# Sixteen more products of zeros in a fused attention and MLP kernel, and its list of steps in another order

## The chip, the cores and the metric

The kernel runs on one core of a Trainium2 chip. The metric is the device time of one execution in microseconds (us), as a median over runs.

## The reference

Eight batches of eight heads, 576 positions, 64 columns a head. Causal attention with a bias from running sums of a gate, then a layer norm, an MLP with ReLU, and the sum:

```python
scores = scale * q @ k.T
cum = cumsum(maximum(s, 0))
scores = where(causal, -1e9, scores + minimum(-(cum[q] - cum[k]), 0))
attn = softmax(scores)
x = concat_heads(attn @ v)                 # 8 x 576 x 512
xn = (x - mean(x)) / sqrt(var(x) + 1e-6) * g_ln
out = x + maximum(xn @ w_ch1, 0) @ w_ch2   # 512 -> 2048 -> 512
```

## The kernel before

The bias is folded into the values: a key's weight is the exponential of its running sum, less a share of the last sum. The sums are scanned on VectorE (DVE), turned on TensorE (PE) and put through an exponential on ScalarE (ACT) into the tile `wt` (steps `relu`, `relur`, `scan`, `wr`, `wT`, `wx`; L244 to L257 and L892 to L920). Each v tile, 128 keys of all heads, is multiplied by it (`vm`, L212), on DVE or on GpSimd (POOL), and `vo` adds the weights themselves as two more columns, so that the row sums come out of the same product.

PE runs everything else as matrix products, in this order for a batch: q and k are brought into the form with the head's columns on partitions; scores of keys by queries, an exponential on ACT out of PSUM, the mask of the diagonal on POOL or in the product; the v products; division by the row sums on DVE. Then the rows of the batch are normalised (`ga` statistics, `la` the normalised tile on DVE), turned (`Da`, a transposing DMA), and multiplied by `w1` and, after ReLU, by `w2`. The last 64 rows of two batches make one mixed tile.

The order of all this is written out by hand, as a list of words, `PLAN` (from L1064), that a loop goes through (L1144). A word is a step with its numbers, and after a colon the engine: A for ACT, D for DVE, P for POOL, S for the SP queue. A step appends its instructions to the engines' queues; each engine works its queue in order and waits where data or a buffer is missing. So the list sets the order on each engine, and on each queue of DMAs: SP issues the v loads (`lv`), the row loads of later batches (`lr`) and the transposing DMAs; POOL issues the loads of pairs (`lp`, k then q, with a cast, L158) and of weights (`w1`, `w2`, 512 KB each, L233 to L240), between its own arithmetic. The words `U` and `u` take the next unit from a queue of MLP work (`run_units`, L691): four products of 512 columns, with the ReLU on DVE or on ACT; the first five units of batch 0 are pieces for one tile of rows. A unit is PE's filling work; there are 293 in both lists.

The start differs from the rest. Batches 0 to 2 are loaded as pairs of heads and turned on PE (`F.k.g`, `F.q.g` for pair g: 12 products, L276), then copied out of PSUM (`G`, L296). The pairs 0 to 3 are batch 0, and pair 0 comes through two f32 loads (`lf`, `cf`). Batch 0 is worked by tiles of queries: `S.t.n.mask` scores into two banks (L761), `x.t.n.i` the exponential (L789), `V.t.g` the v product for half of the heads (L807), `N` its division (L823), `B` and `L` statistics and normalised tile, `X` and `y` its transpose on PE and the copy, `M.c.t.j` a piece of the first MLP product with the weights of chunk c (L849), `r` its ReLU. `sd`, `se`, `sm` are the scores of the last 64 rows against themselves, their exponential on ACT and their mask on POOL (L375 to L398), `tk` the copy of the k tails for them, `me` a memset that it needs, `Z` the v products of the last rows. `fv` fills the tail of a v tile with zeros. From batch 1 on pairs are worked as bursts (`B2`, L402) with `bx`, `bm`, `Y` and `K` for exponential, mask, v products and division.

PSUM has eight banks. Up to the step `t6` two of them are `m` (pieces of the MLP), four `s` (scores) and two `t` (transposes of pairs and tiles, the turned sums, v products of batch 0). After `t6` there are two `m` (v products, outputs of the MLP) and six `s`. The step `W.n` (`keep_warm`, L704) lets PE multiply a tile of zeros n times, 512 columns each, into a bank that nobody reads:

Of the kernel before, what the change touches and what calls it, by code (L numbers as in the profile page):

```python
# [30 lines left out]
def fast_path(  # L31
# [672 lines left out]
    def keep_warm(n):  # L704
        w = ptile("t", [P, 512], "idle")
        for _ in range(n):
            nc.tensor.matmul(w, lhsT=zeros[:, 0:P], rhs=zeros, start=True, stop=True)
# [657 lines left out]
```

## Time and profile before

| What | us |
|---|---|
| median of three runs | 348.97 (348.58 to 349.32) |
| the profiled execution | 348.05 |
| its span, first to last instruction | 346.6 |
| PE busy in the span | 329.8 |

A profile is one execution. Engines are PE, PEld (the loading of weights into PE, which overlaps), DVE, ACT, POOL and SP; a q behind a name is its queue. A row of a timeline has the start, the busy time of the group, the engine, the line, the operation, what it writes and reads, the count, and in brackets the idle time ahead of it with what ended it. The granted clock is the share of full speed that the tensor engine's throttle let through.

### The profile page before, as it was taken

To read this page: it belongs to the slowest core of one execution; us is meant where nothing else is said; L and a number is where in the kernel's file an instruction comes from. 1 tells how busy PE (TensorE), PEld (TensorE's weight loads), DVE (VectorE), ACT (ScalarE), POOL (GpSimd) and SP (SyncE) were. 2 spreads that over 40 slices of the span, in tenths; PEclk is the share of its full clock that TensorE was granted. 3 is DMA by queue.
4 is the path that set the end of the run, shared out by engine and by line. 5 is a ranking of instruction groups with operands and counts; after the bars stand their busy time and mean duration, and the time that the engine had idled before them with its cause. 6 is when DMAs were issued, how large, how long until landed. Compare 5 with 4: busy or idle time off the path is not lost.

```text
span 346.6 us, 8106 instructions
## 1 busy us (share of the span) xinstructions
PE 329.8 (95%) x3143; PEld 178.2 (51%) x3169; DVE 223.0 (64%) x613; ACT 168.0 (48%) x312; POOL 146.9 (42%) x270
## 2 busy tenths in 40 slices
PE   5888899999999999999999999999999999999994
PEld 2667756555554555545554544554545444444443
DVE  3577859877698697747775768684867745025412
ACT  3685399775654667434762463363732202402500
POOL 6196968663777843664584173422240001000000
PEclk9569999999999999999999999999999999999998
DMA  8999999999999999889959924900140060021022
GB/s 161 207 198 224 207 204 206 178 204 261 169 207 253 195 213 229 181 186 199 230 151 206 220 46 109 220 25 2 62 121 3 0 166 32 0 77 61 1 60 65
DMA packets 140186, 49.76 MB, mean 144 GB/s; under 512 B 126000, under 2 KB 135984, under 8 KB 140144
## 3 DMA queue, kind: packets, MB, share of 16 engines
q1 hardware_dynamic: 130336, 40.69, 56.1%
q0 software_dynamic: 8880, 7.70, 13.9%
q10 hardware_dynamic: 928, 0.82, 0.9%
q8 instruction: 25, 0.41, 0.5%
q14 instruction: 17, 0.14, 0.1%
HBM read 37.11 MB, written 9.44 MB: 134 GB/s over the span
## 4 chain that ended last, share of the span: by engine, by line
PE 84%; DMA 4%; POOL 4%; DVE 3%; ACT 3%; issue 2%; POOLq 0%
PE py L629 35%; PE ph L610 34%; PE pot L442 5%; DMA qp<-in_q_dram 4%; PE sa L409 2%; ACT er L416 2%; PE sc L409 2%; PE pott L483 2%; PE sb L409 1%; POOL v_bf L215 1%; PE trp L289 1%; DVE v_bf L215 1%; ACT kq L138 1%; PE trp L282 1%; POOL kp L160 1%
## 5 line engine op out<-in xcount | busy, mean ns | idle before, releaser
L629 PE MATMUL py<-w_bf,hT 128*128 128x512 bf16 (+2 forms) x582 | 128.7, 367 | 2.2 <-issue 0.5
L610 PE MATMUL ph<-xT,w_bf 128*128 128x512 bf16 x480 | 109.2, 379 | 0.9 <-DVE hT L867 0.7
L602 ACT ACTIVATE hT<-ph 128x512 bf16<-128x512 f32 x78 | 46.8, 599 | 105.2 <-PE ph L610 104.1
L629 PEld LDWEIGHTS <-hT 128*128 128x128 bf16 x608 | 55.8, 98 | 60.0 <-DVE xb L461 0.3
L610 PEld LDWEIGHTS <-w_bf 128*128 128x128 bf16 x544 | 51.6, 98 | 58.8 <-issue 0.8
L353 POOL TENSOR_SCALAR_AFFINE_SELECT er<-er 128x256 bf16<-128x256 bf16 x112 | 46.5, 435 | 48.3 <-ACT er L416 34.3
L600 DVE TENSOR_SCALAR hT<-ph 128x512 bf16<-128x512 f32 x58 | 39.7, 688 | 25.0 <-PE ph L610 23.4
L641 DVE SCALAR_TENSOR_TENSOR yo<-py,rstd,xb 128x512 f32<-128x512 f32 x32 | 24.0, 749 | 37.5 <-PE py L629 28.7
L416 ACT ACTIVATE er<-sc 128x512 bf16<-128x512 f32 x56 | 33.3, 622 | 15.4 <-PE sc L409 15.1
L416 ACT ACTIVATE er<-sa 128x512 bf16<-128x512 f32 x56 | 33.8, 620 | 11.4 <-PE sa L409 11.0
L416 ACT ACTIVATE er<-sb 128x512 bf16<-128x512 f32 x56 | 33.8, 621 | 6.9 <-PE sb L409 4.9
L534 POOL TENSOR_TENSOR rstd<-rstd,mhalf 128x4 f32<-128x4 f32 (+1 forms) x8 | 9.2, 1145 | 48.2 <-DVE rstd L533 45.8
L215 POOL TENSOR_TENSOR v_bf<-rowtmp,wt 128x512 bf16<-128x512 f32 (+1 forms) x21 | 22.2, 1064 | 13.1 <-ACT wt L915 9.0
L442 PEld LDWEIGHTS <-er 128*128 128x128 bf16 x560 | 22.3, 97 | 9.7 <-DVE xb L461 0.9
L442 PE MATMUL pot<-v_bf,er 128*128 128x66 bf16 x560 | 25.3, 193 | 0.5 <-DVE xb L461 0.4
L200 POOL CAST kq<-rowtmp 128x512 bf16<-128x512 f32 (+1 forms) x30 | 19.5, 661 | 14.3 <-DMA rowtmp<-in_k_dram 14.3
L519 DVE BATCH_NORM_STATS2 stats<-xb 128x6 f32<-128x128 f32 (+1 forms) x84 | 24.8, 326 | 0.4
L461 DVE TENSOR_TENSOR xb<-pot,rinvs 128x256 f32<-128x256 f32 x56 | 23.8, 424 | 1.9
L560 DVE SCALAR_TENSOR_TENSOR xn<-xb,mv,gb 128x512 bf16<-128x512 f32 x28 | 22.9, 820 | 1.0
L409 PEld LDWEIGHTS <-kq 64*128 64x128 bf16 x448 | 14.3, 94 | 12.9 <-issue 6.7
L459 DVE TENSOR_REDUCE sums<-pot 128x4 f32<-128x8 f32 x56 | 8.8, 158 | 17.7 <-PE pot L442 17.2
L215 DVE TENSOR_TENSOR v_bf<-rowtmp,wt 128x512 bf16<-128x512 f32 (+1 forms) x19 | 17.4, 919 | 1.6 <-DMA rowtmp<-in_v_dram 1.6
(124 smaller groups left out, 320.3 us busy)
## 6 DMA issues: line engine op xcount, KB each, us to landing
rowtmp<-in_v_dram SPq DMA_DIRECT2D x32, 256.0 KB, 4.7
out_dram<-yo SPq DMA_DIRECT2D x32, 256.0 KB, 2.5
rowtmp<-in_k_dram SPq DMA_DIRECT2D x20, 256.0 KB, 4.0
rowtmp<-in_q_dram SPq DMA_DIRECT2D x20, 256.0 KB, 4.7
w_bf<-in_moe_w_ch_dram POOLq DMA_DIRECT2D x8, 512.0 KB, 9.9
kp<-in_k_dram POOLq DMA_DIRECT2D x11, 144.0 KB, 6.7
qp<-in_q_dram POOLq DMA_DIRECT2D x11, 144.0 KB, 7.0
rowtmp<-in_v_dram SPq DMA_DIRECT2D x8, 128.0 KB, 4.6
```

Source lines behind the costliest of these rows:

```text
L215: e.tensor_tensor(out=v_bf[b % 2][0:pn, t, :, 0:D], in0=loaded.pop(("v", b, t))[0:pn], in1=wt[0:pn, t, b, :].unsqueeze(2).to_broadcast([pn ...
L353: nc.gpsimd.affine_select(out=out, in_=out, compare_op=ALU.is_ge, fill=0.0, base=0, pattern=pattern, channel_multiplier=-1,)
L409: nc.tensor.matmul(a, lhsT=lhsT, rhs=rhs, start=True, stop=True)
L416: nc.scalar.activation(out=er[:, 2 * n % 4 + i, o : o + 512], in_=bank["B", n].pop((name, i)), func=ACT.Exp, scale=scale,)
L442: nc.tensor.matmul(pot[:, t, :], lhsT=e[:, o : o + P], rhs=v_bf[b % 2][:, kb, h, :], start=(kb == 0), stop=(kb == t),)
L461: nc.vector.tensor_tensor(out=xb[b][:, :, h * D : (h + 1) * D], in0=pot[:, :, 0:D], in1=rinv.unsqueeze(2).to_broadcast([P, NF, D]), op=ALU ...
L519: nc.vector.bn_stats(out=st[b][:, t, part, :], in_=x_tiles(b)[t][:, lo:hi])
L600: nc.vector.tensor_scalar_max(out=dst, in0=ph, scalar1=0.0)
L602: nc.scalar.activation(out=dst, in_=ph, func=ACT.Relu)
L610: nc.tensor.matmul(ph, lhsT=w1_bf[:, kd, fb * P : (fb + 1) * P], rhs=xT[:, :, kd, :], start=(kd == 0), stop=(kd == KD - 1),)
L629: nc.tensor.matmul(py[t], lhsT=hT[:, fb, t * P : (t + 1) * P], rhs=w2_bf[:, fb, c0:c1], start=(fb == 0), stop=(fb == FB - 1),)
L641: nc.vector.scalar_tensor_tensor(out=yo, in0=py[t], scalar=rs, in1=x[:, c0:c1], op0=ALU.mult, op1=ALU.add)
```

## The change

The bank of the zero product goes from `t` to `m`, and the list has another order. Beside W.9 there are now W.2 four times, W.3 once and W.1 five times, 16 products more. Some steps go to another engine: of the v tiles twelve words (`vm`, `vo`) go from POOL to DVE and eleven from DVE to POOL, several copies `G`, `y` and `O2` change between ACT and DVE, and four units have their ReLU on DVE instead of ACT. Otherwise both lists hold the same words. Shown are the lines of the list up to the first burst, with those of two of the transposing DMAs that are spoken of further on; the rest of the list changes its order in the same manner.

```diff
     def keep_warm(n):
-        w = ptile("t", [P, 512], "idle")
+        w = ptile("m", [P, 512], "idle")
         for _ in range(n):
             nc.tensor.matmul(w, lhsT=zeros[:, 0:P], rhs=zeros, start=True, stop=True)
...
     PLAN = """
-        f.0 mT c.0 I lf.k:S lf.q:A f.5 W.9 c.1 f.10 relur.2 relu.0 cf.q:D F.q.0 G.q.0:A lv.0.0:S O relur.1 lp.1
-        F.k.1 lp.2 f.2 scan.0 f.1 G.k.1:D cf.k:A qu.1 F.q.1 G.q.1:A F.k.0 G.k.0:A lv.0.1:S F.k.2 G.k.2:A S.1.0.1
-        lp.3 x.1.0.1 F.q.2 scan.1 scan.2 w1.1 wr F.k.3 G.q.2:A lv.0.3:S F.q.3 G.q.3:A wT wx vm.0.0:P g x.1.0.0
-        qu.2 G.k.3:D fv.0 S.0.0.1 S.1.1.1 x.0.0.0 vo.0:D w1.0 lv.0.2:S vm.0.1:D x.0.0.1 V.0.1 N.0.1 x.1.1.0
-        x.1.1.1 me B.0.1 S.2.0.1 S.4.0.0 V.1.0 N.1.0 V.0.0 tk.0 lv.0.4:S lv.1.0 x.2.0.0 x.4.0.1 N.0.0 x.4.0.0
-        x.2.0.1 S.4.1.0 x.4.1.0 lv.1.1 x.4.1.1 S.2.2.1 x.2.2.0 lp.7 vm.0.2:P qu.3 V.1.1 lv.1.3 qu.4 vm.0.3:P
-        S.2.1.1 lp.6 L.0 x.2.2.1 x.2.1.1 X.0 x.2.1.0 S.3.1.1 x.3.1.0 y.0:A B.1.0 S.3.0.1 x.3.0.1 V.2.0 vm.0.4:P
-        N.1.1 V.2.1 sd.0 L.1 X.1 N.2.1 x.3.1.1 S.3.3.1 M.0.0.0 lr.3.0 x.3.0.0 N.2.0 B.1.1 vm.1.0:P L.2 M.0.0.1
-        M.0.0.3 y.1:A M.0.1.0 lv.1.2 M.0.0.2 r.0.0:D V.3.0 N.3.0 M.0.1.2 S.3.2.1 A.1 lv.2.0 X.2 y.2:D se.0
-        M.0.1.3 x.3.3.1 M.0.1.1 M.0.2.2 r.0.1:D x.3.3.0 x.3.2.1 M.0.2.1 lp.4 B.0.0 M.0.2.3 x.3.2.0 M.0.2.0 V.3.1
-        N.3.1 L.3 r.0.2:A sm.0 Z.0 z.0 lp.5 F.k.4 F.q.4 w1.2 U G.k.4:A X.3 lp.8 F.k.6 y.3:D G.q.4:A w2.0 vo.1:P
-        B.2.0 G.k.6:A U u vm.1.1:P vm.1.3:D w1.3 cr.3.0.1 B.2.1 F.k.5 G.k.5:D La.3 F.q.5 G.q.5:D vm.1.2:P fv.1 U
-        u U u lp.9 t6 B.3.0 F.k.7 G.k.7:A lv.1.4 B.3.1 tk.1 F.q.6 G.q.6:D B2.4 A.0 bx.4.1 bx.4.3 w2.3 bx.4.0 U
...
-        cr.4.2.0 u u la.2.0 ga.2.0.3 bx.12.1 bm.12.1 cr.4.4.0 lv.4.1 bm.12.2 bm.12.3 se.3 la.2.3 Da.2.0 B2.13
...
-        bm.30.0 ga.6.1.2 la.6.2 U bx.30.3 bx.30.4 la.6.3 Da.6.0 U Y.29.1 K.29.1 B2.31 bx.31.3 u bx.31.2 bx.31.1
...
+        f.0 W.9 W.2 W.2 lf.k:S lf.q:A f.5 I c.1 lp.1 c.0 cf.k:A lv.0.1:S lv.0.0:S relur.2 fv.1 f.10 lp.2 me
+        F.k.1 f.2 O relur.1 cf.q:D F.q.0 lv.0.4:S W.3 F.q.1 F.k.2 relu.0 G.q.0:A W.1 G.q.1:A lv.0.2:S F.k.0
+        G.k.0:A W.1 scan.0 G.k.1:D lp.3 W.1 mT F.k.3 scan.1 lv.0.3:S G.k.2:D W.1 scan.2 G.k.3:A tk.0 lv.1.0
+        S.2.0.1 wr m F.q.2 wT G.q.2:D qu.1 wx g S.1.0.1 x.1.0.1 x.1.0.0 F.q.3 G.q.3:D w1.1 vo.0:D S.0.0.1
+        vm.0.3:D x.2.0.1 S.1.1.1 x.2.0.0 x.0.0.0 W.1 vm.0.1:P S.4.1.0 vm.0.0:D x.0.0.1 V.0.0 N.0.0 lv.1.3
+        x.1.1.0 x.1.1.1 V.1.0 w1.0 x.4.1.1 lp.4 x.4.1.0 V.0.1 S.4.0.0 N.1.0 lp.5 x.4.0.0 S.2.1.1 x.2.1.0 W.2
+        N.0.1 vm.0.2:P vm.1.0:P V.1.1 N.1.1 qu.2 L.1 x.2.1.1 B.1.1 x.4.0.1 L.0 S.3.0.1 V.2.0 x.3.0.0 W.2 S.2.2.1
+        x.3.0.1 X.1 lv.1.1 lr.3.0 qu.3 B.0.1 x.2.2.0 y.1:A sd.0 x.2.2.1 V.2.1 M.0.1.3 S.3.1.1 lv.1.2 x.3.1.0
+        M.0.1.1 N.2.0 f.1 X.0 se.0 sm.0 M.0.1.2 M.0.1.0 N.2.1 L.2 B.2.1 lp.6 B.1.0 F.q.4 G.q.4:D S.3.3.1 X.2
+        lv.1.4 y.0:A M.0.0.2 S.3.2.1 y.2:A M.0.2.3 fv.0 lp.8 r.0.1:A x.3.1.1 V.3.0 N.3.0 M.0.0.0 x.3.3.0
+        vm.0.4:P F.q.5 M.0.2.2 G.q.5:D x.3.3.1 x.3.2.1 M.0.0.3 x.3.2.0 M.0.2.0 V.3.1 lv.2.0 N.3.1 M.0.2.1
+        r.0.2:A M.0.0.1 r.0.0:D w1.2 F.k.6 G.k.6:A F.k.4 G.k.4:D B.2.0 L.3 Z.0 z.0 B.0.0 lp.7 cr.3.0.0 F.k.5
+        G.k.5:A u B.3.0 X.3 y.3:A vo.1:P u u u cr.3.0.1 A.0 u u U La.3 B.3.1 vm.1.2:D w1.3 vm.1.1:P t6 O2.q.8:D
+        F.q.7 F.k.7 G.q.7:A G.k.7:A B2.4 bx.4.1 lp.9 w2.1 A.3 U U w2.0 vm.1.3:D bx.4.0 vm.1.4:D bx.4.2 bx.4.3
...
+        bm.14.2 bm.13.3 K.12.1 bx.14.5 la.2.3 lr.4.2 cr.4.2.0 u U Da.2.0 lv.4.3 bx.14.1 bm.13.1 u sm.3 Y.13.0
...
+        bm.29.2 Y.29.0 bx.30.3 la.6.2 U U K.29.0 bx.30.5 bx.30.4 bx.30.2 u u u B2.31 bx.31.0 bx.31.2 la.6.0
+        la.6.3 Da.6.0 u u bx.31.4 bm.31.0 sm.7 bm.30.0 U U u bm.29.3 Y.29.1 bx.31.3 bx.31.5 K.29.1 ga.7.0.1
...
```

More of the change, by code (lines that the diff above doesn't have):

```diff
@@ new lines, in fast_path @@
+        vm.4.1:P U bm.15.0 u bm.15.2 lv.4.0 Y.14.0 K.14.0 Y.14.1 K.14.1 lr.5.0 lv.4.4 U vo.4:D u u u bm.15.1
+        Y.15.1 lv.5.2 qm lr.6.4 cr.5.2.1 lr.6.1 B2.16 bx.16.1 cr.5.4.0 lv.5.4 bx.16.0 sm.4 Z.3 ga.3.1.3 z.3
+        bx.16.3 bx.16.5 ga.3.0.0 bx.16.4 lv.5.0 u U cr.5.4.1 Y.15.0 K.15.0 K.15.1 ga.3.2.3 vm.4.0:P bx.16.2
+        bm.16.0 bm.16.2 cr.5.2.0 vo.5:D u ga.3.1.2 bm.16.3 vm.4.3:P u u lv.6.0 u ga.3.0.3 u ga.3.2.4 Y.16.0
+        bm.16.1 ga.3.1.1 lv.5.3 Da.1.4 B2.17 bx.17.1 bx.17.0 bx.17.3 Y.16.1 K.16.0 ga.3.1.0 bx.17.4 ga.3.1.4
@@ new lines, in fast_path @@
+        K.17.1 ga.4.0.0 lv.5.1 Y.18.1 U bm.19.2 U bx.19.1 u K.18.1 vm.5.0:P U lr.6.3 bm.19.0 lv.6.2 lv.6.1 u
+        Y.18.0 K.18.0 ga.4.0.1 Y.19.0 K.19.0 B2.20 lr.6.2 bx.20.1 Z.4 bx.20.4 vm.5.3:D lv.6.4 bx.20.2 la.3.4
+        bx.20.0 vm.5.1:D bm.19.1 bx.20.5 bx.20.3 U U u z.4 U cr.6.4.1 u cr.6.4.0 u u bm.20.0 ga.4.0.2 Y.19.1
+        K.19.1 bm.20.2 ga.4.2.1 Y.20.0 bm.20.1 K.20.0 tr.6.4.5 cr.6.3.0 bm.20.3 ga.4.2.3 B2.21 lr.7.0 bx.21.1
+        Y.20.1 Da.3.4 u bx.21.0 u ga.4.1.0 lv.7.3 cr.6.2.0 bx.21.3 ga.4.2.0 K.20.1 u U tr.6.0.2 La.7 la.4.0
@@ new lines, in fast_path @@
+        lv.7.4 B2.24 bx.24.0 bx.24.3 ga.5.0.3 La.5 ga.5.1.1 bx.24.2 z.5 bm.24.0 vm.6.3:D vo.6:D bx.24.4 ga.5.0.2
+        Y.23.0 K.23.0 ga.5.2.1 bx.24.1 lr.7.2 cr.7.2.0 vm.6.1:P U cr.7.0.0 U lr.7.3 bx.24.5 U ga.5.2.2 u
+        ga.5.2.3 u U bm.24.2 ga.5.0.1 ga.5.1.4 U U u bm.24.1 ga.5.1.3 ga.5.2.4 u cr.7.4.0 u B2.25 la.5.3 U
+        ga.5.1.2 bx.25.1 bx.25.4 Y.24.0 lv.7.0 u cr.7.4.1 cr.7.0.1 cr.7.1.0 la.5.1 lv.7.1 sm.6 cr.7.1.1 K.24.0
+        tr.7.0.2 u bx.25.5 bm.25.3 bx.25.0 la.5.2 vm.6.4:P bx.25.3 u u lv.7.2 cr.7.3.0 bx.25.2 bm.24.3 Y.24.1
@@ L1143, in fast_path @@
+        U u U
     """
```

109 lines of the change are left out of this document (46 added, 63 removed).

## The prediction

> **What bounds the kernel now.** I read the page first, for the engine with no room.
>
> ```profile
> span 346.6 us, 8106 instructions
> PE 329.8 (95%) x3143; PEld 178.2 (51%) x3169; DVE 223.0 (64%) x613; ACT 168.0 (48%) x312; POOL 146.9 (42%) x270
> ```
>
> The tensor engine is busy 95% of the span; the rest have room on average. Next, the table by stretches: start, length, then busy time of PE, weight loads, DVE, ACT and POOL, the granted clock, the DMA share.
>
> ```profile
> 0.00:9.40 9.40, 5.02 (x35) 1.91 (x37) 3.79 (x11) 3.30 (x6) 5.84 (x15) 1.00 0.84 164
> 9.40:13.84 4.44, 3.94 (x72) 3.17 (x73) 1.61 (x5) 3.06 (x5) 0.00 (x0) 0.51 1.26 195
> 13.84:19.60 5.76, 5.76 (x81) 4.48 (x82) 3.75 (x11) 4.33 (x8) 3.71 (x5) 0.50 1.02 197
> 19.60:23.40 3.80, 2.81 (x59) 2.15 (x57) 3.20 (x14) 3.28 (x7) 3.68 (x7) 0.95 1.07 192
> 23.40:26.40 3.00, 3.00 (x43) 2.21 (x42) 1.55 (x4) 3.00 (x7) 2.98 (x5) 0.50 1.26 235
> 26.40:44.71 18.31, 16.25 (x342) 13.59 (x340) 15.19 (x42) 8.16 (x16) 13.72 (x22) 1.00 1.27 216
> 44.71:60.00 15.29, 14.04 (x196) 8.49 (x194) 10.57 (x38) 14.85 (x31) 11.72 (x24) 1.00 1.23 205
> 60.00:320.00 260.00, 257.31 (x2203) 130.74 (x2226) 175.78 (x462) 122.82 (x229) 105.26 (x196) 1.00 0.67 141
> 320.00:342.00 22.00, 21.54 (x132) 11.40 (x132) 7.51 (x31) 5.17 (x9) 0.00 (x0) 1.00 0.15 37
> ```
>
> From 60 us on PE idles 2.69 of 260 us, and 0.46 us in the last stretch: the end comes when PE has done its work. Nothing but the start can be won there. Up to 44.71 us, where the first burst in six banks begins, it is busy 36.78 us (5.02 + 3.94 + 5.76 + 2.81 + 3.00 + 16.25) and idle 7.93. Of the busy time, 12.70 us (3.94 + 5.76 + 3.00) ran at half clock; at full clock it would be some 6.35. Third, the timeline of PE for what held it.
>
> ```profile
> 1.49 4.02 PE L707 MATMUL idle<-hT 128*128 128x512 bf16 x9 [1.49 <-DVE hT L733]
> 7.18 0.45 PE L289 MATMUL trp<-ident,kp 96*64 96x96 bf16 x12 [0.78 <-DMA kp<-in_k_dram]
> 9.37 0.62 PE L289 MATMUL trp<-ident,qp 96*64 96x96 bf16 x12 [1.74 <-DMA qp<-in_q_dram]
> 13.84 0.69 PE L289 MATMUL trp<-ident,qp 96*64 96x96 bf16 x12 [0.25 <-ACT kq L138]
> 17.52 0.43 PE L813 MATMUL pot<-v_bf,er 128*128 128x66 bf16 x4
> 27.75 0.40 PE L593 MATMUL trx<-ident,xn 128*128 128x128 bf16 x4 [0.71 <-DVE xb L829]
> 28.54 1.28 PE L854 MATMUL ph<-xT,w_bf 128*128 128x128 bf16 x20
> 37.09 1.96 PE L854 MATMUL ph<-xT,w_bf 128*128 128x128 bf16 x32
> 39.26 0.42 PE L289 MATMUL trp<-ident,qp 96*64 96x96 bf16 x12
> 39.62 1.96 PE L854 MATMUL ph<-xT,w_bf 128*128 128x128 bf16 x32
> 42.26 1.89 PE L610 MATMUL ph<-xT,w_bf 128*128 128x512 bf16 x8 [0.68 <-DVE hT L867]
> 44.71 0.39 PE L409 MATMUL sa<-kq 64*128 64x512 bf16 x2
> ```
>
> The last q pair of batch 0 is turned at 13.84 us, as its load lands: half clock up to there costs nothing, since PE would only wait. The cold stretches that can matter are the two after it, 5.76 + 3.00 us, 4.4 us at most by halving. The engines around PE come next, from their own timelines: POOL issues the loads of pairs and weights in order with its arithmetic.
>
> ```profile
> 4.80 0.63 POOL L160 DMA_DIRECT2D kp<-in_k_dram  x1
> 6.04 0.78 POOL L235 DMA_DIRECT2D w_bf<-in_moe_w_ch_dram  x1
> 15.81 1.04 POOL L215 TENSOR_TENSOR v_bf<-rowtmp,wt 128x512 bf16<-128x512 f32 x1 [8.99 <-ACT wt L915]
> 17.94 0.75 POOL L235 DMA_DIRECT2D w_bf<-in_moe_w_ch_dram  x1
> 18.73 1.44 POOL L1010 MEMSET c<- 128x1600 bf16 x1
> 20.23 0.84 POOL L142 COPY c<-kq 64x256 bf16<-64x256 bf16 x2
> 24.42 0.69 POOL L160 DMA_DIRECT2D kp<-in_k_dram  x1
> 29.34 0.88 POOL L353 TENSOR_SCALAR_AFFINE_SELECT c<-c 64x512 bf16<-64x512 bf16 x1 [0.27 <-ACT c L393]
> 31.43 0.77 POOL L235 DMA_DIRECT2D w_bf<-in_moe_w_ch_dram  x1
> 15.29 0.44 ACT L915 ACTIVATE wt<-trw 128x320 f32<-128x320 f32 x1
> 20.12 4.51 ACT L790 ACTIVATE er<-st 128x512 bf16<-128x512 f32 x9 [0.77 <-PE pot L813]
> ```
>
> POOL stands 8.99 us waiting for the weights `wt` of the keys, then works without a break. ACT does exponentials back to back, 0.50 us each (4.51 / 9).
>
> **The change, part by part.** The zeros first. One product takes 0.45 us cold (4.02 / 9). The four added at the head start at about 5.5 us, in time that ends with the 0.78 us wait for the first k pair; they cost nothing. The three of W.3 and the five single ones stand among waits for pairs 1 to 3, like the 1.74 us one at 9.37, or ahead of the first v product; nothing again, 0.45 us each if that cover were gone. The two W.2 after the first v products stand on the path: four products, 0.9 us at full clock (1.89 / 8 each, 0.24), 1.8 us at half. That they use the banks of the v products hinders nobody before the first piece of the MLP, and frees the two transpose banks. The transposes of pairs need them: F.q.1 and F.k.2 now come ahead of the copies that empty the banks, so F.q.1 waits for G.k.1 on DVE, behind the clamp and the first scan. Queued behind it is all of PE; by the landing at 9.37, no later than now, the copy is done, so I count nothing.
>
> POOL's queue. The mask waits, the identity comes first: pairs 1 and 2 are issued no later than now, even with the fill of a v tile ahead of pair 2. The memset (1.44) now goes ahead of pair 3, whose issue moves from 4.80 to about 6.4. But pair 3 is at the end of a queue that delivers up to 13.84 already, so I take the arrival as unchanged; bounds: 0.5 us earlier to 1.6 us later. Then tail copies of k (0.84) wait for the copy of k pair 3 on ACT; behind them are the gain, w1.1, a v tile and w1.0. w1.1 thus moves from 6.04 to about 15.1, w1.0 from 17.94 to about 17. Their landing:
>
> ```profile
> w_bf<-in_moe_w_ch_dram POOLq DMA_DIRECT2D x1, 512.0 KB, 12.2
> w_bf<-in_moe_w_ch_dram POOLq DMA_DIRECT2D x1, 512.0 KB, 7.5
> w_bf<-in_moe_w_ch_dram POOLq DMA_DIRECT2D x1, 512.0 KB, 9.3
> kp<-in_k_dram POOLq DMA_DIRECT2D x1, 144.0 KB, 6.7
> xT<-xn SPq DMA_TRANSPOSE x1, 4.3
> L560 DVE SCALAR_TENSOR_TENSOR xn<-xb,mv,gb 128x512 bf16<-128x512 f32 x28 | 22.9, 820 | 1.0
> ```
>
> These are the issues at 6.04, 17.94, 31.43 and 24.42, a transpose of batch 6, and the group of the normalisations. w1.0 landed in 7.5 us; with w1.1 just ahead, between 7.5 and 12.2, so at 24.5 to 29.2. I take 24.5 to 25, nearest to the row of the same load, since the v loads have the engines to themselves from 7 to 15 us and are out of its way.
>
> The middle of the start. `wt` comes when it does now, 15.3 to 15.75, since the turned sums wait for the same pairs. Of the v tiles, two move to DVE and one from it. PE then waits for the first v tile, behind another on DVE, until about 19, where it now starts at 17.52; but ACT meanwhile has four score tiles to work on, so it isn't starved. From its first v product to its first piece (28.54) PE now has 6.8 us of work at full clock: 2.08 / 2 + 2.81 + 3.00 / 2 + 1.4 (26.4 to 28.54 less the 0.71 idle). The new order has four score tiles and a transposed tile fewer there, some 2.3 us by an estimate of 0.5 a tile, and the four zeros, 0.9: 5.4, so its first piece, M.0.1.3, is due at 24.4. The next wait is new: POOL's mask of the diagonal tails (sm.0) now stands ahead of lp.6, and behind it are lp.6, a fill, lp.8, a v tile and w1.2. It follows the ACT step se.0, which comes after 19 exponentials, one copy and the small f.1: 15.75 + 19 x 0.50 + 0.5 + 0.2 = 25.95, and 0.55 for itself, 26.5. The mask takes 0.88 (29.34): lp.6 is issued at 27.4 against 24.42 now, and lands 6.7 later, at 34.1. That is the wait that comes last on PE: F.k.6 is the gate where now pair 5 was. w1.2 follows at 27.4 + 1.3 + 0.5 + 1.3 + 1.0 = 31.5, the time of now, and lands at 40.8.
>
> From F.k.6 to the first burst PE has five groups of transposes at 0.36 (39.26 to 39.62), 1.8; the tail products and one transposed tile, 44 products, most of half a piece's width or less, where 0.06 us is a piece's product (1.89 / 32): about 1.0; five units of pieces at 0.95 (37.09 to 38.98, two) and two units at 0.91 (42.26 to 44.08): 1.8 + 1.0 + 4.75 + 1.8 = 9.35. The burst begins at 34.1 + 9.4 = 43.5. The sixth unit, the first to need w1.2, is due at 40.9: just in time. Useful PE work ahead of that burst is the same in both lists (seven units, the same score, v and piece steps), so 44.71 - 43.5 = 1.2 us is the gain, and it reaches the end, PE being full behind it.
>
> Later stages: the counts of every step agree but for four units whose clamp goes from ACT to DVE, and v tiles change engines twelve one way, eleven the other. I cost these at nothing, covered by DVE's idle time of 84 us in 260; without cover 0.69 us each. Several transposes of normalised tiles (Da) stand nearer to their first use: a rival below.
>
> The profiled execution took 348.05: the span and 1.45 us around it. Less 1.2 gives 346.85. The median of the three runs is 348.97, 0.92 above; I keep that offset and predict 347.8.
>
> The clock, weighed. In the rows, twelve-matmul transposes with gaps (5.9 to 9.4) were followed by half clock, and dense work from 13.84 to 19.6 by full clock. The Trainium skill ("TensorE: Matmul & The Clock Gate", Part 1) gives a free-running window of about 3.4 us: a window that is not busy enough halves the clock, a busy one restores it. The cold stretches of 10.2 and 3.0 us fit that roughly, not exactly. By rows alone the sum stays at 1.2; by that rule the wait ahead of the first v product could bring the clock down again, a rival below.
>
> **The rivals.** (a) More gain: the clock stays up after 13.84, ACT starts its exponentials a microsecond sooner, and nothing waits for lp.6. Without the wait PE would reach the burst at about 41, 3.7 us early: 345.3. For it: w1.1 out of the early loads; against: the queue before lp.6. 0.17.
>
> (b) No change: the loads set the start. The DMA share is above 1 from 9.4 to 60 us, and the same bytes have to come. The burst then begins within 0.7 us of now: 348.97. 0.10. By the clock rule the wait for the first v product (up to 19) leaves PE cold for 3.4 us of dense work, 1.7 us lost; it delays the scores, se.0 and lp.6 alike, 43.5 + 1.7 = 45.2, and in part lies in ACT's time: about 349.2, also no change. 0.10.
>
> (c) Slower: w1.0 lands late. PE is ready for its first piece at 24.4, and behind it in order stands S.3.1.1, whose exponential is ahead of se.0. For equality lp.6 must be issued by 44.71 - 9.4 - 6.7 = 28.6, so the mask ends, se.0 ends at 27.7, and the piece starts by about 26. From a landing at 26 on, each microsecond is lost. At 28, 2 us: 351.0. For it: two weight loads in a row; against: 7.5 us in the same place. 0.17.
>
> (d) Given back later: the two normalisations of batch 6 and their transpose stand 5.5 us of PE work ahead of their use, now 7.9; batch 2 has 5.9, now 13.0. The transpose takes 4.3, two normalisations 1.6 (2 x 0.82): a wait of 0.4 to 1.2 us at two places, and more if DVE lags; 2 us with no gain at the start: 350.0. 0.10.
>
> **How the numbers follow.** About 0.2%, 0.7 us, is what a measurement here can tell from no change. The forecast case (0.8 to 2 us gained, 347.0 to 348.2) has 0.36. Faster: 0.36 + 0.17 = 0.53; the same: 0.10 + 0.10 = 0.20; slower: 0.17 + 0.10 = 0.27. The range goes from 344.9, case (a) with nearly the whole 4.4 us of cold time, to 350.8, just under case (c); some 0.2 lies outside.
>
> **What would show it.** Right: the first burst near 43.5; w1.1 issued near 15; POOL waiting for se.0, lp.6 behind it near 27.4, and PE waiting for kp at about 34. Clock 1.00 for more of 9.4 to 26.4. Wrong: a wait of the first piece for w1.0; PE idle well over 2.69 us from 60 to 320, at the first products of chunks 2 or 6; or F.k.6 ready when PE comes to it.

## The result and the profile after

| What | before | after |
|---|---|---|
| median, us | 348.9 (348.58 to 349.32) | 359.81 (357.26 to 362.78) |
| the profiled execution, us | 348.05 | 358.21 |
| its span, us | 346.6 | 356.7 |

The ratio is 1.0296, with an interval of 1.0242 to 1.035: slower by 3%, where 347.8 us and a gain were forecast, and outside the range. A ratio compares the executions that came within 1.5% of the fastest of their kernel (three of these four), while a median is over all. Read the page's totals first, then the table by stretches (start, length, busy time of PE, weight loads, DVE, ACT, POOL, granted clock, DMA share, GB/s).

```profile
span 356.7 us, 8179 instructions
PE 336.4 (94%) x3185; PEld 179.1 (50%) x3185; DVE 229.7 (64%) x625; ACT 165.8 (46%) x307; POOL 146.0 (41%) x263
```

```profile
0.00:44.71 44.71, 37.75 (x607) 26.39 (x608) 25.62 (x80) 26.42 (x48) 28.34 (x50) 0.89 1.11 199
44.71:60.00 15.29, 12.55 (x161) 7.02 (x159) 11.30 (x30) 11.49 (x23) 9.74 (x19) 0.89 1.23 205
60.00:80.00 20.00, 16.57 (x180) 9.31 (x181) 15.96 (x42) 9.91 (x17) 8.92 (x14) 0.91 0.65 123
80.00:320.00 240.00, 238.30 (x2065) 120.80 (x2062) 166.94 (x450) 112.02 (x211) 98.95 (x181) 1.00 0.66 140
```

The same stretch of before:

```profile
60.00:80.00 20.00, 19.69 (x201) 10.59 (x203) 16.69 (x43) 14.15 (x25) 12.28 (x22) 1.00 1.02 201
```

From 80 us on PE is as full as it was, idle 1.70 us in 240. The loss is all ahead of that. From 60 to 80 us PE idles 3.43 us where it idled 0.31, and some of its work is at half clock. Together that is 5.1 us of idle time from 60 to 320, where the forecast named "well over 2.69" as a sign of being wrong. I also compared each burst's start with the work that stands ahead of it in the two lists: the first burst is 1.5 us late, the third 1.3, the fourth 3.4, the fifth 9.0, and from there on about 9 to 10. The forecast said that nothing but the start can be won; more was lost behind it.

PE's timeline of after, with the rows that answer to the forecast's steps and the waits between the first and the fifth burst:

```profile
21.17 0.84 PE L813 MATMUL pot<-v_bf,er 128*128 128x66 bf16 x12
28.31 0.38 PE L854 MATMUL ph<-xT,w_bf 128*128 128x128 bf16 x4
36.49 0.45 PE L289 MATMUL trp<-ident,kp 96*64 96x96 bf16 x12
46.20 0.39 PE L409 MATMUL sa<-kq 64*128 64x512 bf16 x2
54.90 0.33 PE L442 MATMUL pot<-v_bf,er 128*128 128x66 bf16 x5 [0.96 <-DVE rinvs L460]
55.98 0.32 PE L442 MATMUL pot<-v_bf,er 128*128 128x66 bf16 x5 [0.75 <-POOL er L353]
67.49 0.46 PE L442 MATMUL pot<-v_bf,er 128*128 128x66 bf16 x10 [1.03 <-DVE xb L461]
73.20 0.32 PE L483 MATMUL pott<-v_bf,er 128*64 128x66 bf16 x8 [2.39 <-DVE yo L641]
```

The longest wait, 2.39 us, is for `yo`, the sum that empties an `m` bank which the tail products (Z.1) need. DVE's and POOL's timelines beside it show why `yo` was late:

```profile
69.46 3.02 DVE L215 TENSOR_TENSOR v_bf<-rowtmp,wt 128x512 bf16<-128x512 f32 x1
72.40 0.74 DVE L641 SCALAR_TENSOR_TENSOR yo<-py,rstd,xb 128x512 f32<-128x512 f32 x1
```

```profile
68.91 0.69 POOL L160 DMA_DIRECT2D kp<-in_k_dram  x1
69.60 0.63 POOL L160 DMA_DIRECT2D qp<-in_q_dram  x1
70.23 0.68 POOL L353 TENSOR_SCALAR_AFFINE_SELECT c<-c 64x512 bf16<-64x512 bf16 x1
70.87 1.05 POOL L215 TENSOR_TENSOR v_bf<-rowtmp,wt 128x512 bf16<-128x512 f32 x1
```

One product of a v tile (vm.2.1, which was POOL's before) takes 3.02 us on DVE. It ends 0.56 us after POOL's product does (70.87 + 1.05 = 71.92; 69.46 + 3.02 = 72.48). Behind it in DVE's queue stands `yo`, and for that PE waits.

In the start, ACT's timeline holds the step that the forecast rested on, the exponentials up to se.0 (L393):

```profile
15.53 0.44 ACT L915 ACTIVATE wt<-trw 128x320 f32<-128x320 f32 x1 [2.11 <-PE trw L911]
16.50 2.06 ACT L790 ACTIVATE er<-st 128x512 bf16<-128x512 f32 x4 [0.53 <-PE st L777]
18.81 1.08 ACT L790 ACTIVATE er<-st 128x512 bf16<-128x512 f32 x2 [0.24 <-PE st L777]
20.10 1.08 ACT L790 ACTIVATE er<-st 128x512 bf16<-128x512 f32 x2 [0.21 <-PE st L777]
22.12 3.29 ACT L790 ACTIVATE er<-st 128x512 bf16<-128x512 f32 x6 [0.93 <-PE pot L813]
...
29.23 0.60 ACT L790 ACTIVATE kq<-st 128x512 bf16<-128x512 f32 x1 [1.19 <-PE st L777]
...
29.81 0.58 ACT L393 ACTIVATE c<-sd 64x512 bf16<-64x512 f32 x1
```

The waits in brackets, 0.53 + 0.24 + 0.21 + 0.93 + 1.19 = 3.1 us, are what the forecast left out. POOL waited for se.0, as forecast, and issued pair 6 behind it, at 31.07 (forecast 27.4). From 9.4 to 26.4 us the granted clock was 0.70, where the same stretch of before had 0.60.

```profile
30.46 0.65 POOL L353 TENSOR_SCALAR_AFFINE_SELECT c<-c 64x512 bf16<-64x512 bf16 x1 [7.99 <-ACT c L393]
31.07 0.69 POOL L160 DMA_DIRECT2D kp<-in_k_dram  x1
```

### The profile page after: what moved, and what is told of

Its sections match the earlier page's. It is cut to its first block, busy times and chain, and to the rows that moved or that the text cites. A ratio compares the mean times of both kernels' runs of the same rounds, so it can differ in the third digit from the quotient of the medians.

```text
span 356.7 us, 8179 instructions
## 1 busy us (share of the span) xinstructions
PE 336.4 (94%) x3185; PEld 179.1 (50%) x3185; DVE 229.7 (64%) x625; ACT 165.8 (46%) x307; POOL 146.0 (41%) x263
## 5 line engine op out<-in xcount | busy, mean ns | idle before, releaser
L629 PE MATMUL py<-w_bf,hT 128*128 128x512 bf16 (+2 forms) x608 | 132.8, 371 | 0.0
L602 ACT ACTIVATE hT<-ph 128x512 bf16<-128x512 f32 x70 | 41.7, 602 | 97.2 <-PE ph L610 96.4
L600 DVE TENSOR_SCALAR hT<-ph 128x512 bf16<-128x512 f32 x66 | 44.3, 686 | 32.1 <-PE ph L610 31.1
L416 ACT ACTIVATE er<-sa 128x512 bf16<-128x512 f32 x56 | 32.7, 608 | 16.1 <-PE sa L409 13.1
L416 ACT ACTIVATE er<-sb 128x512 bf16<-128x512 f32 x56 | 32.8, 611 | 12.3 <-PE sb L409 5.7
L215 POOL TENSOR_TENSOR v_bf<-rowtmp,wt 128x512 bf16<-128x512 f32 (+1 forms) x22 | 23.8, 1083 | 2.1 <-DMA rowtmp<-in_v_dram 1.5
L215 DVE TENSOR_TENSOR v_bf<-rowtmp,wt 128x512 bf16<-128x512 f32 (+1 forms) x18 | 16.5, 926 | 0.1
```

The source lines that it names most:

```text
L215: e.tensor_tensor(out=v_bf[b % 2][0:pn, t, :, 0:D], in0=loaded.pop(("v", b, t))[0:pn], in1=wt[0:pn, t, b, :].unsqueeze(2).to_broadcast([pn ...
L416: nc.scalar.activation(out=er[:, 2 * n % 4 + i, o : o + 512], in_=bank["B", n].pop((name, i)), func=ACT.Exp, scale=scale,)
L600: nc.vector.tensor_scalar_max(out=dst, in0=ph, scalar1=0.0)
L602: nc.scalar.activation(out=dst, in_=ph, func=ACT.Relu)
L629: nc.tensor.matmul(py[t], lhsT=hT[:, fb, t * P : (t + 1) * P], rhs=w2_bf[:, fb, c0:c1], start=(fb == 0), stop=(fb == FB - 1),)
```

## The experiments

Runs of one group shared a chip and its runs of the kernel before (medians 348.15, 348.7, 348.46 and 349.61 us in this order).

### First group: which part of the change

**The zeros alone.** The old list, with the 16 products and the other bank.

```diff
-W.9 ... F.q.1 ... F.k.2 ... F.k.3 ... S.1.1.1 ... S.2.1.1 ... S.3.0.1
+W.9 W.2 W.2 ... W.3 F.q.1 W.1 ... F.k.2 W.1 W.1 ... F.k.3 W.1 ... S.1.1.1 W.1 ... S.2.1.1 W.2 ... S.3.0.1 W.2
```

> The old list with the sixteen products added at the like places and the bank changed. Theory A (the order loses the time, the zeros nearly nothing): within 1 us of the kernel before, since most of them stand in waits for pairs and only the two W.2 after the first v products (0.9 us at full clock) lie on PE's path. Theory B (the zeros lose it: 16 products of 0.22 to 0.45 us on a full engine, 3.5 to 7 us): 4 us or more above the kernel before.

349.91 us, ratio 1.0056 (1.003 to 1.0082). That is 1.8 us over the 348.15 of before, a little more than theory A allowed and well under theory B. The zeros did keep the clock up to the first piece (the table by stretches, and PE's timeline):

```profile
9.40:26.40 17.00, 14.06 (x265) 9.40 (x265) 11.43 (x39) 13.94 (x28) 10.89 (x15) 1.00 1.16 203
```

```profile
26.40:45.30 18.90, 16.77 (x322) 14.17 (x322) 14.04 (x36) 7.36 (x14) 13.31 (x22) 0.91 1.26 211
```

```profile
26.78 1.28 PE L854 MATMUL ph<-xT,w_bf 128*128 128x128 bf16 x20
32.96 0.45 PE L289 MATMUL trp<-ident,kp 96*64 96x96 bf16 x12 [0.61 <-DMA kp<-in_k_dram]
34.31 0.45 PE L289 MATMUL trp<-ident,qp 96*64 96x96 bf16 x12 [0.91 <-DMA qp<-in_q_dram]
45.29 0.39 PE L409 MATMUL sa<-kq 64*128 64x512 bf16 x2
```

The clock was full from 9.4 to 26.4 us, where before had half in most of it, and the first piece came at 26.78 us, 1.8 us ahead of the 28.54 of before. But there PE waited 0.61 and 0.91 us for pairs, and some 3.4 us at half clock followed (the 0.91). The first burst is 0.6 us later than the 44.71 of before. So full clock up to the first piece does not by itself bring the burst forward.

**The order alone.** The new list with no zeros but W.9.

```diff
-f.0 W.9 W.2 W.2 lf.k:S ... W.3 F.q.1 ... W.1 ... W.2 S.2.2.1 ...
+f.0 W.9 lf.k:S ... F.q.1 ... S.2.2.1 ...
```

> The new list without the sixteen products; the nine at the head stay. Theory A: as slow as the changed kernel within 2 us, 357 to 361. Theory B: near the kernel before, 349 to 354.

357.93 us, ratio 1.0291 (1.0258 to 1.0324), the ratio of the whole change. The order loses the time, and in it the zeros cost nothing that can be told.

**The two halves of the order.** The new list up to the first burst with the old order behind it, and the other way round. Words that the other list has ahead of the burst stand just before it.

```diff
-... (new list) F.q.7 F.k.7 G.q.7:A G.k.7:A B2.4 bx.4.1 lp.9 w2.1 ...
+... (new list) F.q.7 F.k.7 G.q.7:A G.k.7:A qu.4 A.1 w2.0 vm.1.3:D lp.9 tk.1 F.q.6 G.q.6:D B2.4 bx.4.1 bx.4.3 w2.3 ... (old list)
```

> The new list up to the first burst (B2.4), then the remaining words in the old order. By the traces the new order is 1.5 us behind at that burst and 9.0 us behind at B2.8, 22 words of PE work later. Theory A1 (the later stretch of the list loses the most): 350 to 352, the 1.5 us of the start and little else. Rival A2 (the start leaves the engines and loads in a state that the rest pays for): 356 or more.

```diff
-... (new list) F.q.7 F.k.7 G.q.7:A G.k.7:A B2.4 ...
+... (old list, W.9 only) F.q.6 G.q.6:D m cr.3.0.0 A.0 O2.q.8:D F.q.7 G.q.7:A B2.4 ... (new list)
```

> The old list up to the first burst, then the remaining words in the new order. Theory A1: 354 to 357, the loss between B2.4 and B2.8 (7.5 us in the traces) without the start's 1.5. Rival A2: within 1.5 us of the kernel before.

352.32 us, ratio 1.0126 (1.009 to 1.0163), and 353.02, ratio 1.015 (1.0111 to 1.0189): 4.2 and 4.9 us over the 348.15 of before. Together some 9, beside the 9.8 of the order alone: the two halves lose apart from each other, and their losses add, as far as these intervals tell. Neither came as expected: the new start costs more than the 1.5 us at the first burst, the new rest less than 7.5. With the old start the long wait is there again, with the same stretched product:

```profile
63.81 0.46 PE L442 MATMUL pot<-v_bf,er 128*128 128x66 bf16 x10 [1.02 <-DVE xb L461]
69.53 0.32 PE L483 MATMUL pott<-v_bf,er 128*64 128x66 bf16 x8 [2.40 <-DVE yo L641]
```

```profile
65.78 3.03 DVE L215 TENSOR_TENSOR v_bf<-rowtmp,wt 128x512 bf16<-128x512 f32 x1
```

### Second group: single causes

**The product moved, later and earlier.** Behind Z.1's division, or behind the division K.6.0, both still on DVE.

```diff
-... lr.3.4 vm.2.1:D O2.k.10:A ... Z.1 z.1 ga.1.2.4 ...
+... lr.3.4 O2.k.10:A ... Z.1 z.1 vm.2.1:D ga.1.2.4 ...
```

> The new list with one word moved: the v product of batch 2, key tile 1, on DVE (vm.2.1) stands behind the division of the last rows of batch 1 (z.1) instead of ahead of the output step of the third unit before it. Theory A1 (that product takes 3.02 us while POOL works without a break, the output step behind it on DVE empties a bank late, and PE waits 2.4 us for the bank): the wait of the last-row products for DVE goes, 2.4 us less than the new list, and up to 4.1 where the half clock of 3.4 us that follows the wait goes too: 353.5 to 356. Rival A3 (the bank is late by some other step): the wait stays, 357 to 361.

```diff
-... K.6.0 A.2 ... lr.3.4 vm.2.1:D O2.k.10:A ...
+... K.6.0 vm.2.1:D A.2 ... lr.3.4 O2.k.10:A ...
```

> The new list with the same word moved the other way, to behind K.6.0 (about 60 us), where POOL is idle for 5.8 us in the changed kernel. Theory A1 with POOL as the cause: the product takes 0.7 to 1.0 us there, and the wait of 2.4 us goes: 353.5 to 356. If the 3.02 us belong to the product itself (its data late): it is as long here, and DVE is held up at 60 us instead.

355.97 us, ratio 1.0147 (1.006 to 1.0233), and 354.09, ratio 1.0144 (1.0055 to 1.0234). In both the product took 0.7 us and the wait of 2.4 us was gone:

```profile
62.92 0.68 DVE L215 TENSOR_TENSOR v_bf<-rowtmp,wt 128x512 bf16<-128x512 f32 x1
```

By the ratios half of the loss went with one word of the list, some 5 us; the intervals leave 2 to 9. One execution of the first kernel took 860 us, and what happened in it is not known.

The second of these runs shows something else as well. Up to the first burst its words are those of the changed kernel, but its clock was full from 9.4 to 26.4 us:

```profile
9.40:26.40 17.00, 12.94 (x248) 8.93 (x248) 13.21 (x43) 12.07 (x23) 8.48 (x12) 1.00 1.15 206
```

```profile
14.93 4.03 ACT L790 ACTIVATE er<-st 128x512 bf16<-128x512 f32 x8
28.65 0.60 ACT L790 ACTIVATE kq<-st 128x512 bf16<-128x512 f32 x1 [3.12 <-PE st L777]
```

```profile
27.32 0.53 PE L854 MATMUL ph<-xT,w_bf 128*128 128x128 bf16 x4 [1.34 <-DMA w_bf<-in_moe_w_ch_dram]
46.69 0.39 PE L409 MATMUL sa<-kq 64*128 64x512 bf16 x2
```

The exponentials began 1.6 us earlier (14.93 against 16.50), and PE came early to its first piece and waited there for w1.0. The burst was not earlier. The same words reached it at 46.20 us (the changed kernel), 46.69 (here), 48.17 (the product later) and 47.20 (a run further on), so the first burst of a single execution can't tell differences under 2 us.

**Scores earlier.** The first scores and their exponentials ahead of the last k pair.

```diff
-... W.1 mT F.k.3 ... g S.1.0.1 x.1.0.1 x.1.0.0 F.q.3 ...
+... W.1 mT S.1.0.1 x.1.0.1 x.1.0.0 F.k.3 ... g F.q.3 ...
```

> The new list with S.1.0.1 and its two exponentials moved ahead of the transposes of k pair 3, near to where the old list has them. Theory S1 (ACT begins its exponentials 4 us later than before, 16.5 against 12.5 us, and ends them 2.7 us later, and the start hangs on that): first exponential by 13.5, last one 1 to 2.5 us earlier, first burst at 44 to 45.2, time 1 to 2.5 us under the new list. Rival S2 (POOL, held up 8 us by the mask sm.0, is what counts): burst at 46.2 as now, no gain.

360.6 us, ratio 1.033 (1.0264 to 1.0396): no gain. The exponentials came at 14.82, but the last k pair at 14.72, and the turned sums only at 17.36; the burst was at 48.6 (48.17 for the unchanged order in an execution with the same clock of 0.60 from 9.4 to 26.4 us). That theory fell.

**The mask later.** POOL's mask of the diagonal tails behind the load of w1.2, so that nothing there waits for se.0.

```diff
-... X.0 se.0 sm.0 M.0.1.2 ... r.0.0:D w1.2 F.k.6 ...
+... X.0 se.0 M.0.1.2 ... r.0.0:D w1.2 sm.0 F.k.6 ...
```

> The new list with the mask of the diagonal tails (sm.0) moved behind the load of w1.2, so that POOL isn't held up: lp.6 issued near 22.5 instead of 31.1. Theory S2: first burst 1.5 us earlier or more, time 1.5 to 3 us under the new list. Theory S1: PE doesn't wait for those loads (no wait for kp at 36 us in the changed kernel), burst within 0.5 us of 46.2, time within 1 us of the new list.

357.46 us, ratio 1.0225 (1.015 to 1.0301). Pair 6 was issued at 23.68 instead of 31.07, and the burst came no earlier, at 48.1: POOL's new wait, which the forecast took for the gate, isn't it. PE waited 1.05 us for weights at its first piece instead. The time, 2.4 us under the changed kernel's median, would have suited S2, but the ratio's interval reaches up to that of the whole change.

### Third group: where the start loses, and whether the product is enough

**Old start, new rest, product moved.**

```diff
-... (old start, new rest) K.6.0 A.2 ... lr.3.4 vm.2.1:D O2.k.10:A ...
+... (old start, new rest) K.6.0 vm.2.1:D A.2 ... lr.3.4 O2.k.10:A ...
```

> The old list up to the first burst, the new order behind it, and the product of v tile 2.1 moved to behind the division K.6.0 (where it took 0.68 us in the run with the whole new list). Theory: of the 5.2 us that the new order behind the first burst cost with the old start, the wait of 2.4 us for the stretched product is 2.4 to 3, so 350 to 351.2. Rival: some other product becomes the stretched one, or the wait passes to the next bank, and the time stays at 352 to 353.5.

350.14 us, ratio 1.0053 (1.0024 to 1.0082), where the same list with the product in its place had 1.015. So by the ratios 3.4 of the 5.2 us are this product's (0.0097 and 0.015 of 348.15), give or take 1.7; some 2 us stay with the other waits of the new rest.

**Old list up to the turned sums, then the new.**

```diff
-f.0 W.9 W.2 W.2 lf.k:S ... (new list)
+f.0 mT c.0 I lf.k:S ... F.q.3 G.q.3:A wT wx (old list) fv.1 me ... (new list, no zeros)
```

> The old list up to the exponential of the turned sums (step wx, about 15 us), then the new order, without the 16 products of zeros. Theory F (the start loses its time in the order of the first transposes and loads, before wt): as good as the old start with the new rest, 352 to 354, first burst 44.5 to 45.5. Rival D (it loses it between wt and the first burst, through the order of scores, masks and loads): as the new order without zeros, 356.5 to 358.5, first burst 46 or later.

359.65 us, ratio 1.0303 (1.025 to 1.0355): no better than the whole new list, and by the median 1.2 us above the rival's range as well. The order of the first transposes and loads by itself isn't what loses.

**Pair 3 and w1.1 early**, as in the old list.

```diff
-... lp.2 me F.k.1 ... lp.3 W.1 mT ... G.q.3:D w1.1 vo.0:D ...
+... lp.2 lp.3 w1.1 fv.1 me F.k.1 ... W.1 mT ... G.q.3:D vo.0:D ...
```

> The new list with the issue of pair 3 and of w1.1 directly behind pair 2, as in the old list, ahead of the fill and the memset. Theory L (pair 3 comes late and w1.1 holds up w1.0): the k pair 3 lands at 11 to 12 instead of 12 to 13, the first piece waits for no weights, first burst 1 to 2.5 us earlier, time 355.5 to 358 beside 359.8 of the new list. Rival F (it is PE's own order up to the turned sums that is slow): within 1.5 us of the new list, 358.5 to 361. The early w1.1 may also slow the v loads and pair 3; then it is slower than the new list.

359.58 us, ratio 1.0328 (1.03 to 1.0356). The exponentials began at 14.65, but the unchanged order began them at 14.93 where the clock was full (0.90 here), so the move gave them 0.3 us at most. And now the v tiles were late behind the early weights, PE waited for the first of them, and the burst came at 48.95:

```profile
21.27 0.53 PE L813 MATMUL pot<-v_bf,er 128*128 128x66 bf16 x12 [3.13 <-DVE v_bf L215]
```

```profile
19.71 1.50 DVE L215 TENSOR_TENSOR v_bf<-rowtmp,wt 128x512 bf16<-128x512 f32 x2 [3.03 <-DMA rowtmp<-in_v_dram]
```

**Pair 0 ahead of pair 2.**

```diff
-W.3 F.q.1 F.k.2 relu.0 G.q.0:A W.1 G.q.1:A lv.0.2:S F.k.0 G.k.0:A W.1
+W.3 F.q.1 relu.0 G.q.0:A F.k.0 W.1 G.q.1:A lv.0.2:S F.k.2 G.k.0:A W.1
```

> The new list with k pair 0, which is there first, turned ahead of k pair 2, as in the old list; only this pair of transposes and copies is exchanged. Theory F: PE works while pair 2 is on its way, the turned sums come 0.4 to 1 us earlier, first burst 0.4 to 1 us earlier, time 358 to 359.5. Rival L: PE waits for pair 3 anyway, no difference over 0.4 us.

358.17 us, ratio 1.0268 (1.0219 to 1.0318). The exponentials began at 14.92; at the first piece PE then waited for w1.0, and the burst came at 46.72. The unchanged order at the same full clock has 14.93, a wait of 1.34 us and 46.69, so the exchange did nothing, as the rival said:

```profile
27.06 0.40 PE L854 MATMUL ph<-xT,w_bf 128*128 128x128 bf16 x4 [1.16 <-DMA w_bf<-in_moe_w_ch_dram]
```

### Fourth group: POOL beside the product, and the parts together

**POOL's neighbours moved**, the product left where it is.

```diff
-... cr.3.1.0 ga.1.1.1 lp.11 ... lp.10 sm.1 qu.5 ... ga.1.2.4 vm.2.3:P La.2 ... to G.q.11:D ...
+... cr.3.1.0 ga.1.1.1 sm.1 lp.11 ... lp.10 qu.5 ... ga.1.2.4 La.2 ... to vm.2.3:P G.q.11:D ...
```

> The new list; the product of v tile 2.1 on VectorE stays where it is, and GpSimd's two operations beside it go elsewhere: the mask sm.1 ahead of lp.11, the product vm.2.3 behind the step to. Theory P (a product on VectorE that begins while GpSimd reads the on-chip memory is held until GpSimd's operation ends, and then takes 0.55 us): it begins beside loads being issued at most, and takes 0.7 to 1.3 us instead of 3.02; the wait of 2.4 us for its successor falls to 0.7 or less, and the time to 355 to 357.5. Rival I (the product is slow by itself at this place, through its own operands): 3.0 us again, wait 2.4, time 358.5 to 361.

356.69 us, ratio 1.0256 (1.0188 to 1.0323). The casts of row tiles moved up into the gap, which I had not thought of; so the product did not fall to the time that I gave, but to 1.75 us:

```profile
69.55 1.75 DVE L215 TENSOR_TENSOR v_bf<-rowtmp,wt 128x512 bf16<-128x512 f32 x1
```

```profile
70.12 0.62 POOL L200 CAST kq<-rowtmp 128x512 bf16<-128x512 f32 x1
```

It ends at 71.30, 0.56 us behind POOL's cast (70.12 + 0.62 = 70.74), and the wait on PE was 1.12 us, where 0.7 or less was expected. Nothing was changed on DVE, so the length of its product is set by what POOL does beside it.

**Pair 0 first, and w1.0 loaded ahead of w1.1.**

```diff
-... F.q.3 G.q.3:D w1.1 vo.0:D ... V.1.0 w1.0 x.4.1.1 ...
+... F.q.3 G.q.3:D w1.0 vo.0:D ... V.1.0 w1.1 x.4.1.1 ...
```

> The new list with k pair 0 turned ahead of pair 2, as in the run before, and with the issues of w1.0 and w1.1 exchanged, so that the weights of the first piece are loaded first. Theory C (once PE comes early, the late weights w1.0 are what holds the first piece, and through PE's order the exponential behind it): no wait for weights at the first piece; the exponential se.0 starts about 1 us before the 28.57 of the run with pair 0 alone, first burst 45.2 to 46, time 356.5 to 357.5 beside 358.2. Rival: the v tiles or the scores are the next wait, right behind: first burst 46.3 to 47, time 357.5 to 359.

359.14 us, ratio 1.0319 (1.0247 to 1.0391). No wait for weights, se.0 at 27.48 instead of 28.57; but then PE waited for q pair 4, which is loaded behind them, half clock followed (0.81 from 26.4 to 44.71 us), and the burst came at 48.1. The next wait was right behind, as the rival had it, but it was for neither the v tiles nor the scores, and burst and time came out beyond the rival's figures too.

```profile
29.31 0.45 PE L289 MATMUL trp<-ident,qp 96*64 96x96 bf16 x12 [1.51 <-DMA qp<-in_q_dram]
```

**All blamed parts repaired**: both of these, the product behind K.6.0, no zeros but W.9.

```diff
-f.0 W.9 W.2 W.2 ... W.3 F.q.1 F.k.2 ... w1.1 ... w1.0 ... K.6.0 A.2 ... lr.3.4 vm.2.1:D ...
+f.0 W.9 ... F.q.1 relu.0 G.q.0:A F.k.0 ... w1.0 ... w1.1 ... K.6.0 vm.2.1:D A.2 ... lr.3.4 ...
```

> The new list with what the runs so far blame taken out: k pair 0 first, w1.0 ahead of w1.1, the product of v tile 2.1 behind the division K.6.0, no products of zeros but the first nine. Theory: the parts add up, 358.2 less 1 (weights), less 3 to 4 (product), less 0.5 to 1.5 (zeros): 351.5 to 353.5, still slower than before by what the other waits of the new order cost. Rival: the waits of the start stand beside each other and not in a row, so that each repaired one shows the next: 354 to 356.

352.44 us, ratio 1.0113 (1.0052 to 1.0174), inside the expected span: by the ratios 6.4 us better than the changed kernel, still slower than before. But the parts did not come as expected, and the sum fits by luck. The first burst came at 46.27, so nothing of the two repairs in the start arrived there. From the first burst to the end of the span this run takes 304.7 us (351.0 less 46.27), the run with the product earlier and nothing else 304.8 (351.5 less 46.69), the changed kernel 310.5 (356.7 less 46.20). All of the gain is the product's, with what follows its wait.

```profile
46.27 0.39 PE L409 MATMUL sa<-kq 64*128 64x512 bf16 x2
```

The table by stretches gives this execution a clock of 1.00 from 9.4 to 26.4 us:

```profile
9.40:26.40 17.00, 14.77 (x220) 11.13 (x216) 10.78 (x35) 10.75 (x21) 8.55 (x12) 1.00 1.11 198
```

The products themselves say otherwise. These are PE's groups of scores in that stretch (count, busy time, mean ns of one), here, in the order without zeros (clock 0.50) and with pair 0 ahead of pair 2 (clock 1.00):

```profile
L767 PE MATMUL st<-kq 64*128 64x128 bf16 x56 | 5.0, 300 | 0.3 <-ACT er L790 0.2
L767 PE MATMUL st<-kq 64*128 64x128 bf16 x56 | 5.0, 299 | 0.3 <-ACT er L790 0.2
L767 PE MATMUL st<-kq 64*128 64x128 bf16 x56 | 3.4, 218 | 0.5 <-ACT er L790 0.5
```

So PE was as slow here as in the order without zeros. The trace of this run holds no record of the clock ahead of 27 us, and the table then shows 1.00. It is a second start at half clock, with the same burst as the other:

```profile
9.40:26.40 17.00, 14.63 (x220) 10.98 (x216) 10.40 (x35) 10.84 (x20) 8.44 (x12) 0.50 1.13 204
```

```profile
46.31 0.39 PE L409 MATMUL sa<-kq 64*128 64x512 bf16 x2
```

No version that was run beats the kernel before.

## Why the prediction was wrong, step by step

**The later stages, the step that failed most.** It was put so: "v tiles change engines twelve one way, eleven the other. I cost these at nothing, covered by DVE's idle time of 84 us in 260; without cover 0.69 us each." The bound of 0.69 us was the length of the product by itself. In its new place one of the eleven tiles that went to DVE took 3.02 us, stood ahead of a sum that frees a bank, and PE, with nothing else in its order, waited 2.39 us. Moving that one product is worth 3.4 us by the ratios with the old start, and 5.2 and 5.3 us with the new one (0.0149 and 0.0152 of 348.9). In the profiles, the 5.7 us between 310.5 and 304.8 from the first burst to the end are the wait of 2.39 and two stretches of half clock of 1.7 us each, which the run with the product earlier does not have. An engine's idle time over 260 us says nothing of one queue at one moment. Shown: the product's length goes with POOL's work beside it (0.68, 1.75 and 3.02 us, as that work is moved, and 3.57 in the run with pair 3 early), and the wait goes with the product (1.12, 2.39 and 2.94 us for the last three, 0.63 less each time). The stretching alone need not cost anything: the kernel before has a product of 2.09 us, at 120.98, and its longest wait on PE from 80 to 320 us is 0.4 us.

In these rows a product that begins while POOL is at work ends 0.56 us after one of POOL's operations. The Trainium skill ("SBUF — State Buffer", Who interferes with whom) has this as a rule: an instruction of VectorE with two inputs in SBUF contends with one of GpSimd that reads SBUF, over ports that one of them locks for itself. The ends in the trace agree (71.92 and 72.48; 70.74 and 71.30), and this is the rule that spoke against the change; I had weighed only the clock's. It doesn't say why the product, which begins beside two issues of loads, isn't through before the mask at 70.23: two products beside such issues in the start took 1.28 us together. That stays open.

**The sum of the exponentials.** "15.75 + 19 x 0.50 + 0.5 + 0.2 = 25.95" took ACT as back to back, though the row of before that gave the 0.50 has itself a wait of 0.77 us ahead of it. ACT began 0.75 us later (16.50) and had 2.6 us of waits behind that (3.1 in all with the 0.53 ahead of the first). So se.0 began at 29.81, the mask at 30.46 and the load of pair 6 at 31.07 instead of 27.4. That makes 29.3 of the measured 29.81. These waits are for PE, which ran at half clock in part of that time. With full clock the first eight came without a wait from 14.93 on, and se.0 began at 29.24 all the same: the exponential ahead of it then waited 3.12 us for scores that stand behind PE's first piece, and the piece for w1.0. That is the link of case (c). The forecast's consequence fell with another step: the mask later showed that the load is not the gate.

**The first piece** was put at 24.4: the first v product at 19 and 5.4 us from there, out of "6.8 us of work at full clock" counted on PE alone. They came at 21.17 and 28.31. The issues ahead of it held (w1.1 at 14.87, forecast 15.1; w1.0 at 17.09, forecast 17). The 2.2 us at the v product go with the clock: at full clock the same words had it at 18.88. The 1.7 us behind it don't: there too it took 7.1 us to the piece, less the wait for weights (27.32 less 1.34 and 18.88), and 1.5 us of that were waits for DVE and ACT (0.70, 0.56 and 0.20), which a count of PE's work leaves out. This also answers case (a) and the two clock cases: with the clock up from 9.4 to 26.4 us the first piece was earlier, but the burst was not, in the old order (45.29) or the new (46.69).

**The gate.** "That is the wait that comes last on PE: F.k.6" was wrong: its row at 36.49 has no wait, and "F.k.6 ready when PE comes to it" was a sign that the forecast itself had named. From it to the burst the forecast had 9.4 us; measured 9.7 (46.20 less 36.49). That term held.

**w1.0** was put at 7.5 us to its landing, the lower of two rows. The two loads took 9.6 us in the median in the changed kernel:

```profile
w_bf<-in_moe_w_ch_dram POOLq DMA_DIRECT2D x2, 512.0 KB, 9.6
```

There PE came so late that it didn't matter; where PE came earlier, case (c) was the next wait (1.34 and 1.16 us above). Behind it stood pair 4, and with w1.1 early the v tiles. Two chains of nearly one length, the exponentials and the loads, end the new start; taking a link out of one shows the other. The clock takes back the rest. From the first piece to the burst PE needs 17.9 us without half clock (28.31 to 46.20, 28.42 to 46.31), 19.3 to 19.7 where the clock was 0.91 from 26.4 to 44.71 us (27.32 to 46.69, 28.75 to 48.09, 27.06 to 46.72), and 22.1 where it was 0.81 (25.98 to 48.06, with the wait of 1.51 in it). At a like clock the new start is 1.3 to 1.4 us behind the old one: 46.31 against 44.99 (old start, new rest) with 0.50 and 0.52 from 9.4 to 26.4 us, and 46.69 against 45.29 with 1.00 there and 0.91 behind. These are single executions. Which of the orders in the 15 to 45 us makes the compute chain longer than in the old list was not tracked down to a single word.

**The zeros** in the new order: costed at 0.9 us, not measurable (1.0291 without, 1.0296 with). In the old order they cost 1.0 to 2.9 us by the interval (0.003 and 0.0082 of 348.15).

**Case (d)**, the transposed tiles, didn't come: no wait from 80 to 320 us is for one.

**The half clock, the term that was missing.** In the changed kernel, 3.4 us of half clock follow the waits at 55 us and again the long wait at 73; by the table's clocks of 0.89 and 0.91 (1 less a half of 3.4 / 15.29, and of 3.4 / 20) that is 1.7 us each at most. The account by stretches closes: 1.5 us at the first burst; 1.5 more idle (2.74 against the 1.25 of before) and 1.7 of clock up to 60 us; 3.1 more idle and 1.7 of clock up to 80: 9.5 of the 10.2 us between the profiled executions. Whether a wait is followed by a cold stretch varies: behind the same 2.40 us wait with the old start there was none, nor behind 2.94 us with pair 3 early. So a wait costs itself, and at times 1.7 us more; with the 2 us by which the first burst moves, it may be why the four runs of the changed kernel lie 5.5 us apart, which no run shows.

## What to carry to other kernels

When work moves from one engine to another, price it at the place where it lands: what runs beside it, what stands behind it in the queue, and which bank or buffer that frees. A start whose loads and exponentials end together isn't shortened by the engine between them; take the chain with its waits, not one engine's work. Before two executions are compared for the clock, look at what one product took in each, and how far the same words spread. A kernel that is full behind its start can still lose there, and a place with no slack to win deserves as close a look as the place where the gain is expected.
